# Per-head 64x64 key-value sums, and half of the first MLP's weight low parts on GpSimd

## The chip, the cores and the metric

One core of a Trainium2 chip runs the whole program. The metric is the device time of one execution in microseconds (us); less is better. The engines are called PE (TensorE's matmuls), PEld (its weight loads), DVE (VectorE), ACT (ScalarE), POOL (GpSimd) and SP (SyncE, which issues the DMAs).

## What is computed

Three stages follow each other: retention attention (linear attention with a decay per head, no softmax), an MLP with the activation h·cos(h), and a second, gated MLP behind an RMS norm.

```
scores = q @ k.T / sqrt(64)                    # 4 batches, 8 heads, 576 positions, 64 per head
ret    = (scores * gamma[h] ** (i - j) for i >= j, else 0) @ v
x      = ret, heads side by side                # 2304 tokens x 512
h      = x @ w_in                               # 512 -> 2048
x      = (h * cos(h)) @ w_out                   # 2048 -> 512
xn     = x / rms(x) * rms_g
out    = (silu(xn @ w_gate) * (xn @ w_val)) @ w_out2    # 512 -> 1536 -> 512
```

## The kernel before, in words

Each of the 4 batches is cut into 5 chunks of positions, four of 128 and one of 64, so there are 20 chunks, counted here from 0. A chunk is handled in two steps. `scores` (lines 238 to 253) scales the values on POOL (L243), makes the 8 heads' score blocks on PE (L248) and masks them on DVE (L251). `values` (lines 255 to 283) first adds the chunk's keys times values to a running sum in PSUM, `total` (L264, for the four full chunks of a batch); then it makes the output bank `po` from the running `state` and the queries (L269, from the second chunk on), copies the new sum into `state` on ACT (L274), adds each head's scores times values (L279), and takes `po` out of PSUM on DVE into `xall` (L282).

Heads go in pairs, since two heads of 64 fill 128 partitions. Before the change L264 multiplies the pair's 128 key columns by the pair's 128 value columns. Of each 128x128 result only the two 64x64 blocks on the diagonal are wanted, and the copy into `state` takes just these.

The first MLP works on f32 numbers split into a high and a low part (fp32r), three matmuls for one: hi·hi, hi·lo, lo·hi (`mm3`, lines 184 to 188). Its weights come as 16 blocks, each with 512 columns of `w_in` and 512 of `w_out`. A block is turned from two 32-bit words per number into f32 by `value1` to `value3` (L131 and L140 on ACT; L135, L136, L141, L142 on DVE), and split by `convert`: ACT writes the high part of all 1024 columns (L158), DVE the low part by a subtraction (the `w` instruction of L123, called by L159; L123 is the helper `minus`, and other subtractions have that line too: `xlo` for the MLP's input and `glo` for its middle). Each step of the first MLP has 12 matmuls into a hidden bank, the cosine gate (L413 and L416 on ACT, L414 and L420 on DVE, then `ghi` on ACT and `glo` on DVE), and 12 matmuls into the output banks three steps later.

The first 9 chunks' `values` come before the MLP's first step. The other chunks run between the MLP's first 8 steps, and the weight blocks are converted three steps ahead of their use. In this part a scheduler sets each engine's order by its own costs, so an edit here can move instructions that it doesn't name. Each engine then works strictly in the order that it was given. From the 16th step on the order on ACT, DVE and POOL is that of the code.

POOL has little else to do: 20 instructions of L243 in the attention and two `glo` much later.

Of the kernel before, what the change touches and what calls it, by code (L numbers as in the profile page):

```python
# [22 lines left out]
F32 = mybir.dt.float32  # L23
# [7 lines left out]
P = 128  # L31
B, H, S, D = 4, 8, 576, 64
# [5 lines left out]
NPAIR = H // 2  # L38
# [37 lines left out]
def body(ctx: ExitStack, tc, qkv, qkr, vr, w1, w2, rg, gq, gk, mask, out):  # L76
    nc = tc.nc
# [19 lines left out]
    psa = att.enter_context(tc.tile_pool(name="psa", bufs=1, space=PSUM, reuse_waits="tile"))  # L97
# [11 lines left out]
    def ps_tile():  # L109
        if "psh" not in late:  # L110
            return psa.tile([P, 512], F32, tag="g", bufs=3, name="g")
        taken[0] += 1
        return hidden_tile() if taken[0] % 2 else acc_tile(KC + taken[0] // 2 % 2)
# [8 lines left out]
    def minus(eng, dst, hi, src):  # L122
        eng.tensor_tensor(dst, src, hi.bitcast(F32), op=ALU.subtract)  # L123
# [6 lines left out]
    def value1(t, words):  # L130
        nc.scalar.activation(t.bitcast(F32), words[..., 1].bitcast(F32), AF.Abs)  # L131

    def value2(t):
        size = t.bitcast(F32)
        nc.vector.tensor_scalar(size, size, LEAST, LARGEST, op0=ALU.max, op1=ALU.min)  # L135
        nc.vector.tensor_scalar(t, t, 3, 0x3FFFFFF8, op0=ALU.logical_shift_left, op1=ALU.bitwise_and)  # L136

    def value3(t, words):
        low, high = words[..., 0], words[..., 1]
        nc.scalar.activation(low, low.bitcast(U32), AF.Copy, scale=2.0 ** -29)  # L140
        nc.vector.scalar_tensor_tensor(t, high, -2 ** 30, t, op0=ALU.bitwise_and, op1=ALU.bitwise_or)  # L141
        nc.vector.tensor_tensor(t, t, low, op=ALU.add)  # L142

    class Block:
# [7 lines left out]
        def convert(self, t):  # L152
            value1(t, self.raw)
            value2(t)
            value3(t, self.raw)
            self.w = self.where.tile([P, 2, 2, 512], F32R, tag="w", name="w")
            z = t.bitcast(F32)
            nc.scalar.copy(self.w[:, :, 0], z)  # L158
            minus(nc.vector, self.w[:, :, 1], self.w[:, :, 0], z)  # L159

        def parts(self, n):
            return self.w[:, n, 0, :], self.w[:, n, 1, :]
# [42 lines left out]
    ld, sc, total = {}, {}, {}  # L205
# [6 lines left out]
    state = ap1.tile([P, NPAIR, P], F32, name="state")  # L212
# [5 lines left out]
    def load(n):  # L218
# [14 lines left out]
        if 0 < n < NCH:  # L233
            gam.append(ap1.tile([P, NPAIR, width(c)], F32, name=f"gam{c}"))
            for p in range(NPAIR):
                nc.scalar.activation(gam[c][:, p, :], gam0[:, p, :width(c)], AF.Copy, scale=later[:, c, p:p + 1])

    def scores(n):
        b, c = chunks[n]
        w = width(c)  # L240
        kt, qt, vv, _ = ld[n]
        v3 = vv[:w].rearrange("p (h d) -> p h d", h=H)
        nc.gpsimd.tensor_tensor(v3, v3, vg_sb[:w, c, :].unsqueeze(2).to_broadcast([w, H, D]), op=ALU.mult)  # L243
        ps = [ps_tile().rearrange("p (h i) -> p h i", h=NPAIR) for _ in range(2)]
        for p in range(NPAIR):
            for hh in range(2):
                r = slice(hh * D, (hh + 1) * D)
                nc.tensor.matmul(ps[hh][:w, p, :w], kt[r, p, :], qt[r, p, :], start=True, stop=True)  # L248
        for hh in range(2):
            s = ap.tile([P, NPAIR, P], F32, tag=f"s{hh}", bufs=2, name=f"s{hh}")  # L250
            nc.vector.tensor_tensor(s[:w, :, :w], ps[hh][:w, :, :w],  # L251
                                    mask_sb[:w, :w].unsqueeze(1).to_broadcast([w, NPAIR, w]), op=ALU.mult)
            sc[n, hh] = s

    def values(n):
        b, c = chunks[n]
        w = width(c)
        _, qt, vv, kk = ld.pop(n)
        if c < NFULL:
            if c == 0:  # L260
                total[0] = psa.tile([P, NPAIR, P], F32, tag="st", name="total")
            for p in range(NPAIR):
                cs = slice(p * P, (p + 1) * P)
                nc.tensor.matmul(total[0][:, p, :], kk[:, cs], vv[:, cs], start=c == 0 and p == 0, stop=True,  # L264
                                 skip_group_check=True)
        po = ps_tile().rearrange("p (a i) -> p a i", a=NPAIR)
        if c > 0:
            for p in range(NPAIR):
                nc.tensor.matmul(po[:, p, :w], state[:, p, :], qt[:, p, :], start=p == 0, stop=False,  # L269
                                 skip_group_check=True)  # L270
        if c < NFULL:
            for hh in range(2):
                r = slice(hh * D, (hh + 1) * D)
                nc.scalar.copy(state[r, :, r], total[0][r, :, r])  # L274
        for p in range(NPAIR):
            for hh in range(2):
                h = 2 * p + hh
                r = slice(hh * D, (hh + 1) * D)
                nc.tensor.matmul(po[r, p, :w], vv[:w, h * D:(h + 1) * D], sc[n, hh][:w, p, :w],  # L279
                                 start=c == 0 and p == 0, stop=True, skip_group_check=True)  # L280
        t0 = b * S + c * P
        nc.vector.tensor_tensor(xall[:, :, t0:t0 + w], po[:, :, :w], gam[c], op=ALU.mult)  # L282
        del sc[n, 0], sc[n, 1]
# [16 lines left out]

    fetch(1)
    scores(0)
    for n in range(PRO):
        fetch(n + AHEAD)
        scores(n + 1)
        values(n)
        if n == 3:
            split_x(ORDER_A[0])
            blocks1[0].convert(temps())
# [315 lines left out]
    for i in range(LAST + LAG):  # L625
# [12 lines left out]
        if i < LAST:  # L638
            t, f = steps[i]
            ps = hidden(t, f)  # L640
            if f == NF1 - 1 and i + 1 < LAST:
                split_x(ORDER_A[ORDER_A.index(t) + 1])
            gate_cos(t, f, ps, (lambda: scores(more[0] + 1)) if more and more[0] + 1 < N else None,
                     nc.vector if i < NF1 or i >= 3 * NF1 or begun(i) is not None else nc.gpsimd,
                     piece_steps(begun(i), max(valued, default=None)) if begun(i) is not None or valued
                     else other_steps() if i >= LAST - NF1 else iter(range(5)))
        elif i >= LAST:
            for engine in "ADADDD":
                pull(engine)
        if i >= LAG:  # L650
            out_t(*steps[i - LAG])
        if more:
            values(more[0])
            if more[0] + 2 < N:
                scores(more[0] + 2)
            if len(more) > 1:
                values(more[1])
            chunk += len(more)
# [249 lines left out]
```

## Time and profile before

| what | value |
|---|---|
| median of 3 runs | 932.84 us (932.81 to 936.48) |
| the profiled execution, its own time | 929.44 us |
| its span in the profile | 927.7 us |
| PE busy, share of the span | 900.8 us, 97% |
| DVE busy | 619.5 us, 67% |
| ACT busy | 461.9 us, 50% |
| POOL busy | 28.5 us, 3% |
| granted TensorE clock | 1.00 (2.4 GHz) |

A busy PE is not a PE at its peak: matmuls overlap, and their ends are modelled. So for PE the starts of instructions say more than the busy time. An f32 matmul stands in the trace as two instructions: four matmuls of L264 are eight rows. Times inside the program are counted from the span's start.

### The profile page before, as it was taken

To read this page: it belongs to the slowest core of one execution; us is meant where nothing else is said; L and a number is where in the kernel's file an instruction comes from. 1 tells how busy PE (TensorE), PEld (TensorE's weight loads), DVE (VectorE), ACT (ScalarE), POOL (GpSimd) and SP (SyncE) were. 2 spreads that over 40 slices of the span, in tenths; PEclk is the share of its full clock that TensorE was granted. 3 is DMA by queue.
4 is the path that set the end of the run, shared out by engine and by line. 5 is a ranking of instruction groups with operands and counts; after the bars stand their busy time and mean duration, and the time that the engine had idled before them with its cause. 6 is when DMAs were issued, how large, how long until landed. Compare 5 with 4: busy or idle time off the path is not lost.

```text
span 927.7 us, 12893 instructions
## 1 busy us (share of the span) xinstructions
PE 900.8 (97%) x4996; PEld 790.4 (85%) x4996; DVE 619.5 (67%) x1022; ACT 461.9 (50%) x815; POOL 28.5 (3%) x27
## 2 busy tenths in 40 slices
PE   7989999999999999999998899999999999999998
PEld 6777888888887888988887799999888999999997
DVE  3999989678888887768656666675456446333332
ACT  4656566676556665367443444444432334322222
POOL 2321100000000000000000000000000000000000
PEclk9999999999999999999999999999999999999999
DMA  8956451035524443202044466666744555755531
GB/s 328 400 201 225 156 230 66 25 113 193 173 88 159 146 150 125 69 1 102 1 160 180 176 252 250 250 267 249 249 183 176 205 209 214 265 207 209 206 134 68
DMA packets 34732, 163.72 MB, mean 176 GB/s; under 512 B 4080, under 2 KB 5232, under 8 KB 23792
## 3 DMA queue, kind: packets, MB, share of 16 engines
q1 hardware_dynamic: 34672, 162.91, 48.6%
q8 instruction: 39, 0.64, 0.3%
q14 instruction: 21, 0.17, 0.1%
HBM read 123.57 MB, written 39.32 MB: 176 GB/s over the span
## 4 chain that ended last, share of the span: by engine, by line
PE 76%; DVE 16%; ACT 5%; issue 2%; DMA 1%; SPq 0%; ACTq 0%; DVEq 0%
PE h L738 27%; PE acc L710 15%; PE acc L186 8%; PE acc L187 7%; PE acc L188 7%; PE h L187 3%; PE h L188 3%; PE h L186 3%; DVE t L141 1%; DVE r L420 1%; DVE t L142 1%; DVE w L123 1%; DVE r L414 1%; DVE s L251 1%; DVE glo L123 1%
## 5 line engine op out<-in xcount | busy, mean ns | idle before, releaser
L738 PE MATMUL h<-w 128*128 128x384 f32 x1224 | 230.0, 337 | 8.7 <-DVE sg L758 4.2
L738 PEld LDWEIGHTS h<-w 128*128 128x128 f32 x1224 | 215.0, 188 | 16.6 <-DVE sg L758 5.5
L710 PE MATMUL acc<-w,shi 128*128 128x512 f32 x432 | 134.3, 392 | 0.0
L186 PE MATMUL acc<-ghi,w 128*128 128x512 f32 (+1 forms) x320 | 117.3, 373 | 2.8 <-ACT xall L612 1.7
L745 ACT COPY s<-h 128x384 f32<-128x384 f32 x108 | 51.8, 479 | 133.3 <-PE h L738 133.2
L187 PE MATMUL acc<-glo,w 128*128 128x512 f32 (+1 forms) x320 | 117.6, 369 | 0.1
L188 PE MATMUL acc<-ghi,w 128*128 128x512 f32 (+1 forms) x320 | 117.3, 368 | 0.0
L710 PEld LDWEIGHTS acc<-w,shi 128*128 128x128 f32 x432 | 80.1, 188 | 13.5
L758 DVE TENSOR_TENSOR sg<-s,h 128x384 f32<-128x384 f32 x54 | 29.9, 553 | 87.5 <-PE h L738 48.2
L416 ACT ACTIVATE r<-r,half_pi 128x512 f32<-128x512 f32 (+1 forms) x80 | 54.5, 681 | 66.0 <-DVE r L414 65.6
L710 PE MATMUL acc<-w,slo 128*128 128x512 f32 x216 | 85.4, 396 | 0.0
L123 DVE TENSOR_TENSOR glo<-r,ghi 128x512 fp32r<-128x512 f32 (+1 forms) x78 | 49.8, 639 | 33.2 <-ACT ghi L422 31.3
L186 PEld LDWEIGHTS acc<-ghi,w 128*128 128x128 f32 x320 | 59.4, 188 | 14.5 <-ACT xall L612 2.7
L770 ACT CAST shi<-v 128x384 fp32r<-128x384 f32 x72 | 37.1, 515 | 68.6 <-DVE v L766 68.6
L422 ACT CAST ghi<-r 128x512 fp32r<-128x512 f32 (+1 forms) x80 | 46.2, 577 | 48.2 <-DVE r L420 47.0
L188 PEld LDWEIGHTS acc<-ghi,w 128*128 128x128 f32 x320 | 60.3, 188 | 10.1
L187 PEld LDWEIGHTS acc<-glo,w 128*128 128x128 f32 x320 | 60.3, 188 | 10.0 <-DVE glo L123 0.3
L765 DVE TENSOR_TENSOR v<-s,h 128x384 f32<-128x384 f32 x54 | 29.8, 552 | 53.5 <-PE h L738 40.9
L123 DVE TENSOR_TENSOR slo<-v,shi 128x384 fp32r<-128x384 f32 x72 | 40.1, 557 | 36.7 <-ACT shi L770 36.7
L738 PE MATMUL h<-b,w 128*128 128x384 f32 x288 | 56.7, 337 | 0.0
L187 PE MATMUL h<-xlo,w 128*128 128x512 f32 (+1 forms) x148 | 54.3, 367 | 0.1
L188 PE MATMUL h<-xhi,w 128*128 128x512 f32 (+1 forms) x148 | 54.2, 366 | 0.0
(104 smaller groups left out, 1517.1 us busy)
## 6 DMA issues: line engine op xcount, KB each, us to landing
w<-s SPq DMA_DIRECT2D x24, 1024.0 KB, 4.8
raw<-w_dram SPq DMA_DIRECT2D x36, 512.0 KB, 4.2
w<-w SPq DMA_DIRECT2D x18, 1024.0 KB, 5.1
w<-s SPq DMA_DIRECT2D x24, 768.0 KB, 6.5
raw<-w_dram SPq DMA_DIRECT2D x16, 1024.0 KB, 6.7
x<-qkv_dram SPq DMA_DIRECT2D x15, 1024.0 KB, 9.3
s<-w SPq DMA_DIRECT2D x12, 1024.0 KB, 4.8
s<-w SPq DMA_DIRECT2D x12, 768.0 KB, 3.6
```

The lines of the kernel that those rows point to most:

```text
L123: eng.tensor_tensor(dst, src, hi.bitcast(F32), op=ALU.subtract)
L186: nc.tensor.matmul(dst, a[0], b[0], start=start, stop=False)
L187: nc.tensor.matmul(dst, a[0], b[1], start=False, stop=False)
L188: nc.tensor.matmul(dst, a[1], b[0], start=False, stop=stop)
L416: nc.scalar.activation(r, r, AF.Sin, bias=half_pi, scale=1.0)
L422: nc.scalar.copy(hi, r)
L710: nc.tensor.matmul(acc, (hi, hi, lo)[k][:, c], w[:, u, (0, 1, 0)[k], :], start=start and u == 0 and k == 0, stop=stop and u == 1 and k == 2)
L738: nc.tensor.matmul(bank, a[:, wp], xp[:, c], start=start and kc == 0 and n == 0, stop=kc == 1 and n == 2, skip_group_check=True)
L745: nc.scalar.copy(t, alpha)
L758: nc.vector.tensor_tensor(t, s, bank, op=ALU.add)
L765: nc.vector.tensor_tensor(t, s, bank, op=ALU.add)
L770: nc.scalar.copy(hi, t)
```

## The change

Two edits. The sum of keys and values is made head by head: eight matmuls of 64 key columns by 64 value columns, each into its own half of the partitions, in place of four of 128 by 128; `total` shrinks to 64 columns per pair, and the copies into `state` read it accordingly. And of each weight block's low part DVE makes only the `w_in` half, POOL the `w_out` half.

```diff
@@ class Block, convert @@
             nc.scalar.copy(self.w[:, :, 0], z)
-            minus(nc.vector, self.w[:, :, 1], self.w[:, :, 0], z)
+            minus(nc.vector, self.w[:, 0, 1], self.w[:, 0, 0], z[:, 0])
+            minus(nc.gpsimd, self.w[:, 1, 1], self.w[:, 1, 0], z[:, 1])
...
+    half = lambda hh: slice(hh * D, (hh + 1) * D)
...
@@ values @@
-                total[0] = psa.tile([P, NPAIR, P], F32, tag="st", name="total")
+                total[0] = psa.tile([P, NPAIR, D], F32, tag="st", name="total")
             for p in range(NPAIR):
-                cs = slice(p * P, (p + 1) * P)
-                nc.tensor.matmul(total[0][:, p, :], kk[:, cs], vv[:, cs], start=c == 0 and p == 0, stop=True,
-                                 skip_group_check=True)
+                for hh in range(2):
+                    h = 2 * p + hh
+                    cs = slice(h * D, (h + 1) * D)
+                    nc.tensor.matmul(total[0][half(hh), p, :], kk[:, cs], vv[:, cs], start=c == 0 and p == 0,
+                                     stop=True, skip_group_check=True)
...
-                nc.scalar.copy(state[r, :, r], total[0][r, :, r])
+                nc.scalar.copy(state[half(hh), :, half(hh)], total[0][half(hh)])
```

The new code has three lines more ahead of `scores` and two more in `values`, so L243 becomes L246, L264 becomes L269, L269 becomes L274, L282 becomes L285; L123 to L142 keep their numbers.

The scheduler's order moves with it, at three places.

**POOL, the attention and the first MLP's weights.** `x` is a chunk's values being scaled, `w` a weight block's low part. Before, the second half of POOL's attention work:

```order
12 L243 TENSOR_TENSOR x<-x,gk_sb 128x512 x4
13 L243 TENSOR_TENSOR x<-x,gk_sb 64x512
14 L243 TENSOR_TENSOR x<-x,gk_sb 128x512 x4
15 L243 TENSOR_TENSOR x<-x,gk_sb 64x512
16 L123 TENSOR_TENSOR glo<-r,ghi 128x512 x2
```

With the change:

```order
18 L246 TENSOR_TENSOR x<-x,gk_sb 128x512
19 L123 TENSOR_TENSOR w<-t,w 128x512
20 L246 TENSOR_TENSOR x<-x,gk_sb 128x512 x2
21 L123 TENSOR_TENSOR w<-t,w 128x512
22 L246 TENSOR_TENSOR x<-x,gk_sb 64x512
23 L123 TENSOR_TENSOR w<-t,w 128x512
24 L246 TENSOR_TENSOR x<-x,gk_sb 128x512 x2
25 L123 TENSOR_TENSOR w<-t,w 128x512
26 L246 TENSOR_TENSOR x<-x,gk_sb 128x512 x2
27 L123 TENSOR_TENSOR w<-t,w 128x512
28 L246 TENSOR_TENSOR x<-x,gk_sb 64x512
29 L123 TENSOR_TENSOR w<-t,w 128x512 x7
```

Of the 16 `w` instructions nine now stand between the scalings, so that a later chunk's scaling is queued behind a weight block, and seven come after the last chunk's.

**DVE, around the last three attention chunks.** `xall` with `gam_142`, `gam_149` and `gam_159` are the outputs of chunks 17, 18 and 19. Before:

```order
132 L123 TENSOR_TENSOR w<-t,w 128x2x512
133 L123 TENSOR_TENSOR glo<-r,ghi 128x512
134 L135 TENSOR_SCALAR t<-t 128x1024
135 L136 TENSOR_SCALAR t<-t 128x1024
136 L282 TENSOR_TENSOR xall<-g,gam_142 128x4x128
137 L251 TENSOR_TENSOR s_1183<-g,mask_sb 64x4x64
138 L251 TENSOR_TENSOR s_1185<-g,mask_sb 64x4x64
139 L141 SCALAR_TENSOR_TENSOR t<-raw,t 128x1024
140 L142 ISA t<-raw,t 128x2048
141 L282 TENSOR_TENSOR xall<-g,gam_149 128x4x128
```

With the change:

```order
134 L423 TENSOR_TENSOR r<-g,r 128x512
135 L141 SCALAR_TENSOR_TENSOR t<-raw,t 128x1024
136 L123 TENSOR_TENSOR glo<-r,ghi 128x512
137 L142 ISA t<-raw,t 128x2048
138 L285 TENSOR_TENSOR xall<-g,gam_142 128x4x128
139 L254 TENSOR_TENSOR s_1252<-g,mask_sb 64x4x64
140 L254 TENSOR_TENSOR s_1254<-g,mask_sb 64x4x64
141 L123 TENSOR_TENSOR w<-t,w 128x512
142 L285 TENSOR_TENSOR xall<-g,gam_149 128x4x128
```

A block's L141 and L142 have moved from behind chunk 17's output to ahead of it, and a `w`, now of 512 columns, from behind chunk 18's output to ahead of it.

**PE, the first two chunks.** `total` is the sum of keys and values. Before:

```order
12 L279 MATMUL g<-s_138,x 64x128
13 L264 MATMUL total<-x 128x128 x2
14 L248 MATMUL g<-x 128x128 x8
15 L264 MATMUL total<-x 128x128 x2
16 L269 MATMUL g<-x,state 128x128 x4
```

With the change:

```order
12 L282 MATMUL g<-s_138,x 64x128
13 L269 MATMUL total<-x 64x64 x5
14 L251 MATMUL g<-x 128x128 x8
15 L269 MATMUL total<-x 64x64 x3
16 L274 MATMUL g<-x,state 128x128 x4
```

The place is the same; four matmuls of 128 by 128 have become eight of 64 by 64. In both orders 156 matmuls of the first MLP stand ahead of the last chunk's last attention matmul.

## Rows read from the trace of the kernel before

**Rows 1.** Windows: busy us and instructions per engine, clock, DMA share, GB/s.
```profile
21.00:120.00 99.00, 93.80 (x856) 77.84 (x854) 96.36 (x124) 58.76 (x83) 20.97 (x16) 1.00 0.63 239
130.00:165.00 35.00, 35.00 (x156) 28.93 (x155) 34.26 (x44) 24.27 (x31) 0.00 (x0) 1.00 0.35 136
```

**Rows 2.** Timeline of PE, the last chunks: start us, us, what, idle before.
```profile
115.38 1.05 PE L264 MATMUL total<-x 128*128 128x128 f32 x8
116.27 1.06 PE L269 MATMUL g<-x,state 128*128 128x128 f32 x8
117.25 1.09 PE L279 MATMUL g<-s,x 128*64 128x128 f32 x16
118.28 0.68 PE L248 MATMUL g<-x 64*64 64x64 f32 x16
...
120.43 1.16 PE L269 MATMUL g<-x,state 128*128 128x128 f32 x8 [0.38 <-DVE xall L282]
...
129.07 0.68 PE L279 MATMUL g<-s,x 64*64 64x64 f32 x16
129.68 0.50 PE L186 MATMUL acc<-ghi,w 128*128 128x512 f32 x1
```

**Rows 3.** Chain that ended last, in order of time: start us, us, what.
```profile
14.83 0.68 PE total L264 x4
...
58.46 0.68 PE g L248 x8
...
83.15 1.09 PE total L264 x8
...
86.20 0.69 DVE xall L282
```

**Rows 4.** Timeline of DVE while POOL is idle, 111 to 119 us.
```profile
111.93 1.21 DVE L123 TENSOR_TENSOR w<-t,w 128x1024 fp32r<-128x1024 f32 x1
113.06 1.21 DVE L142 CUSTOM_DVE_ANT_0 t<-raw,t 128x2048 uint16<-128x2048 uint16 x1
...
117.76 0.68 DVE L123 TENSOR_TENSOR glo<-r,ghi 128x512 fp32r<-128x512 f32 x1
118.36 0.69 DVE L135 TENSOR_SCALAR t<-t 128x1024 f32<-128x1024 f32 x1
```

**Rows 5.** Timeline of DVE and POOL, 99.5 to 105 us.
```profile
99.93 1.37 POOL L243 TENSOR_TENSOR x<-x,gk_sb 128x512 f32<-128x512 f32 x1 [12.26 <-DMA x<-qkv_dram]
...
100.31 2.07 DVE L123 TENSOR_TENSOR w<-t,w 128x1024 fp32r<-128x1024 f32 x1
...
102.30 1.21 DVE L142 CUSTOM_DVE_ANT_0 t<-raw,t 128x2048 uint16<-128x2048 uint16 x1
102.42 2.00 POOL L243 TENSOR_TENSOR x<-x,gk_sb 128x512 f32<-128x512 f32 x1 [1.12 <-DVE w L123]
...
103.44 0.68 DVE L414 SCALAR_TENSOR_TENSOR r<-r,g 128x512 f32<-128x512 int32 x1
```

**Rows 6.** Groups of 0 to 180 us (count | busy us, mean ns); L243's min/median/max ns.
```profile
L141 DVE SCALAR_TENSOR_TENSOR t<-raw,t 128x1024 int32<-128x1024 int32 x16 | 21.3, 1329 | 0.2
...
L142 DVE CUSTOM_DVE_ANT_0 t<-raw,t 128x2048 uint16<-128x2048 uint16 x16 | 20.4, 1277 | 0.1
L123 DVE TENSOR_TENSOR w<-t,w 128x1024 fp32r<-128x1024 f32 x16 | 20.4, 1273 | 1.3 <-ACT w L158 1.1
...
L136 DVE TENSOR_SCALAR t<-t 128x1024 int32<-128x1024 int32 x16 | 12.6, 785 | 0.2
...
L123 DVE TENSOR_TENSOR xlo<-xall,xhi 128x512 fp32r<-128x512 f32 x8 | 6.2, 810 | 0.7 <-ACT xhi L180 0.7
...
L243 POOL TENSOR_TENSOR x<-x,gk_sb x20: 1037/1068/1997, 7.1 to 109.9; 128x512 f32<-128x512 f32 x16, 64x512 f32<-64x512 f32 x4
```

**Rows 7.** Timeline of ACT and PE, 88 to 96 us: a weight block and chunk 15.
```profile
88.92 1.05 ACT L158 CAST w<-t 128x1024 fp32r<-128x1024 f32 x1 [0.72 <-DVE t L142]
...
95.88 1.16 PE L264 MATMUL total<-x 128*128 128x128 f32 x8
```

More of the change, by code (lines that the diff above doesn't have):

```diff
@@ L272, in values @@
             for hh in range(2):
-                r = slice(hh * D, (hh + 1) * D)
-                nc.scalar.copy(state[r, :, r], total[0][r, :, r])
+                nc.scalar.copy(state[half(hh), :, half(hh)], total[0][half(hh)])
         for p in range(NPAIR):
@@ L277, in values @@
                 h = 2 * p + hh
-                r = slice(hh * D, (hh + 1) * D)
-                nc.tensor.matmul(po[r, p, :w], vv[:w, h * D:(h + 1) * D], sc[n, hh][:w, p, :w],
+                nc.tensor.matmul(po[half(hh), p, :w], vv[:w, h * D:(h + 1) * D], sc[n, hh][:w, p, :w],
                                  start=c == 0 and p == 0, stop=True, skip_group_check=True)
```

## The prediction

> **What bounds the kernel now.** I read the windows first, then the two timelines of PE and DVE, then the chain of waits, and last the groups of instructions of the first 180 us. Both edits touch only the attention and the first MLP's weight blocks; no instruction of either lies behind the first MLP's first 16 steps. In the windows the reader is to see three stretches. From 21 to 120 us DVE is busy 96.4 of 99 us, and PE 93.8: both are nearly full [rows 1]. From 130 us on PE is busy all the time, 35.00 of 35 [rows 1]. So the end of the program moves with one thing: the moment at which the last attention chunks let PE go on. The two orders have the same 156 MLP matmuls ahead of the last chunk's last attention matmul, so what PE has left after that point is the same.
>
> That moment hangs on DVE: chunk 18's first matmul on PE stands 0.38 us for the output that DVE copies out for chunk 17 [rows 2]. The chain of waits lies on PE from 58.46 us to 86.20, where DVE takes it over [rows 3], and on DVE in the stretches ahead of and behind that one, from 21 and to 120 us. The old sums of keys and values (L264) are in it in seven places, the first and the last of which are shown [rows 3]: two before 21 us with 8 instructions, five in PE's stretch with 24. These 32 are the work of four chunks of 16.
>
> **Part 1, what DVE saves.** Starts are the measure, since the shown durations overlap: a low part of 1024 columns holds DVE from 111.93 to 113.06, 1.13 us; one of 512 columns (`glo`, same operation and types) from 117.76 to 118.36, 0.60 us [rows 4]. Each block thus saves DVE 0.53 us. Up to chunk 17's output both orders hold ten blocks' low parts: -5.3 us. But the new order has one block's L141 and L142 ahead of that output which stood behind it before; L142 shows the same 1.21 us as the whole low part [rows 4], so I take 1.13 for each: +2.3 us. Up to chunk 18's output the orders differ by the low parts alone, ten whole ones (11.3 us) against eleven halves (6.6 us): -4.7 us.
>
> **Part 2, what POOL's new work costs DVE.** On POOL the operation takes at least 1.04 us for 128x512, and the longest L243 took 2.00 [rows 6]. POOL has the time: it is busy 21 of 99 us [rows 1]. The price is on DVE. At 99.93 us POOL starts a scaling that lasts until 101.30; DVE's low part starts at 100.31 and takes 2.07 us in place of 1.21, about as much longer as the two overlap [rows 4, 5]. At 102.30 it is the other way round: DVE is first with L142, and POOL's scaling takes 2.00 us [rows 5]. L414, which reads one input from PSUM, runs 0.68 us in the midst of that scaling, not slowed [rows 5]. So a DVE instruction that takes both inputs from SBUF and a POOL instruction exclude each other, and one that reads PSUM passes.
>
> How much does one POOL instruction cost DVE on the average? Against undisturbed durations (1.21 us for the large ones, 0.69 for L136 as for L135, 0.68 for `xlo` as for `glo` [rows 4]) the means are longer by 0.12 us for L141, 0.07 for L142, 0.06 for the low part, 0.10 for L136 (16 of each) and 0.13 for `xlo` (8 of them) [rows 6]: 1.9 + 1.1 + 1.0 + 1.5 + 1.0 = 6.5 us. Of the 20 scalings 16 lie after 21 us, where DVE is full [rows 1], so one costs 0.41 us. The bounds for a `w` on POOL are 0 (only PSUM readers beside it) and 1.04 (none). I take 0.41, since these rows are of the same engine, shape and stretch. Ten blocks up to chunk 17's output: +4.1 us (0 to 10.4); eleven up to chunk 18's: +4.5.
>
> So DVE is at -5.3 + 2.3 + 4.1 = +1.1 us at chunk 17's output and at -4.7 + 4.5 = -0.2 at chunk 18's. Which of them sets the pace I can't tell from the rows, so I take the middle, +0.4.
>
> The Trainium skill speaks against this half of the change: SBUF — State Buffer, section Who interferes with whom, says that VectorE and GpSimd share a port pair under an exclusive lock, so that a VectorE instruction with two SBUF inputs and a GpSimd one that reads SBUF block each other entirely. By that rule the trace agrees (2.07 us against 1.21), and it reads as a full 1.04 us per block wherever no PSUM reader is beside it, which is the second rival below.
>
> **Part 3, the sums of keys and values.** Before, a chunk's L264 holds PE from 115.38 to 116.27, 0.89 us [rows 2]. The new form is 16 instructions with 64 weight columns, 64 moving columns and all 128 rows, two heads in turn into the two halves of the partitions. The nearest row is L279 of a short chunk: 16 instructions, 64 weight and 64 moving columns, the same two halves, but 64 rows; with the step to the next work it takes from 129.07 to 129.68, 0.61 us [rows 2]. The other neighbour has 128 rows and 64 weight columns, but 128 moving columns: 117.25 to 118.28, 1.03 us [rows 2]. The change per chunk lies between -0.28 and +0.14 us; I take -0.28, since what differs in that row (the number of rows summed over) doesn't set the time in the full-size forms either: L264 and L269, 128 rows both, and L279's pair of halves all stand near 0.11 us per 128 columns [rows 2]. For the four chunks that lie on the chain: -1.1 us. For all 16 it would be -4.5, but under DVE's stretches PE then only waits longer.
>
> The Trainium skill has a rule on this: TensorEngine Tiling (Array Packing), section Key Properties, says that changing the tiling mode drains TensorE. The trace agrees in part: from L269 to L279, which goes from whole to half columns, it is 0.98 us where L264 to L269 is 0.89 [rows 2], so 0.09 per change; the 0.61 us above already has one such step in it.
>
> **Part 4, what costs nothing.** POOL's queue: a chunk's scaling now stands behind a block's `w`, which waits for ACT's high part. The tightest place is chunk 15. ACT ends the high part at 89.97 us, so with `w` and the scaling at 1.04 us each the values are ready at about 92.1; PE first uses them at 95.88 [rows 7]. If that cover of 3.8 us went, the sum of chunk 15 and its output would be late by as much as ACT is. The `w_out` half is needed three steps after the `w_in` half. The seven blocks after the attention run under a full PE [rows 1]. The copies into `state` have the same size.
>
> **The sum.** +0.4 - 1.1 = -0.7 us. The profiled execution took 929.44 us, so 928.7; on the median of the runs, 3.4 us above it, 932.1 us. About 0.5% (4.7 us) is what a measurement of this kernel can tell from no change.
>
> **Rivals.**
> 1. *PE sets the pace, and the gain is had in full.* For: PE is nearly as full as DVE from 21 to 120 us, and the scheduler has dealt the work anew on both. Then all 16 chunks count, -4.5 us, and if half of the lock's cost falls beside PSUM readers, DVE's sum at chunk 17's output is -5.3 + 2.3 + 2.05 = -1.0 and PE's waits for it shrink by as much: about -5.5, that is 927.3 us. Against: DVE's stretches in the chain are longer, some 71 us of the first 120 against PE's 28 from 58.46 to 86.20 [rows 3].
> 2. *The lock costs more than the low part was worth.* Every `w` on POOL starts the moment ACT's high part is done, when DVE's next work is mostly the next block's L135 to L142, all reading SBUF. At a full 1.04 us per block: -5.3 + 2.3 + 10.4 - 1.1 = +6.3 us, 939.1 us. It decides from 0.88 us per block on, where the sum passes +4.7. For: the pairs at 100 and 102 us. Against: the mean over 16 scalings is less than half of that.
> 3. *The halves don't go side by side.* Then 16 instructions at L264's 0.11 us each take 1.78 us a chunk, +0.89 us: +3.6 us for the four chunks on the chain, more as PE becomes the bound; about +5 with DVE's +0.4, 937.8 us. Against: L279's halves do go side by side [rows 2].
>
> **How the numbers follow.** The forecast has 0.55, rival 1 0.26, rival 2 0.15, rival 3 0.04. The forecast's own range, with the lock at 0.15 to 0.75 us per block and Part 3 at both ends, is 929 to 937. The whole reaches down to 925.5 to hold rival 1, and up to 938, short of rival 2. Faster by over 0.5% has 0.27 (rival 1 and a little of the forecast's edge), slower by over 0.5% 0.18, no change 0.55.
>
> **What would show it.** In the profile of the changed kernel: `w` on DVE near 0.60 us from start to start, and L141, L142, L135 and L136 with larger means than before by 0.41 us per POOL instruction in sum; a chunk's sum of keys and values at about 0.6 us on PE; DVE still full from 21 to 120 us; chunk 19's output within 2 us of 129.8; PE full from there on. The prediction is wrong if chunk 19's output comes 4 or more us earlier or later, if PE waits for POOL, or if PE loses time after 130 us, where I see none.

## The result, and the profile after

The changed kernel is slower: 941.28 us (median of 6 runs, 938.47 to 942.26) against 932.83 us for the kernel before beside it (6 runs, 930.24 to 936.48). The ratio of the runs is 1.0084, with a 95% interval of 1.0064 to 1.0104: +7.8 us (6.0 to 9.7), where no change (932.1 us) was forecast. The time is above the range, and its sign is the one that had 0.18.

The profiled execution took 942.26 us, its span is 940.1 us. It is 1.0 us above the median of its kernel, and that of the kernel before was 3.4 us below its own, so some 4.4 us of the distance between the two profiles is the spread of the runs. I read it in the order in which the kernel before was read. First the windows of the changed kernel (busy us and instructions of PE, PEld, DVE, ACT and POOL, then clock, DMA share, GB/s):

```profile
21.00:120.00 99.00, 88.41 (x887) 71.03 (x887) 89.94 (x116) 55.41 (x77) 35.65 (x24) 0.91 0.65 238
40.00:80.00 40.00, 33.69 (x297) 27.18 (x298) 32.03 (x42) 22.42 (x30) 12.09 (x8) 0.85 0.49 180
142.00:177.00 35.00, 35.00 (x156) 28.98 (x155) 33.62 (x40) 22.02 (x29) 8.30 (x5) 1.00 0.34 135
```

The same 40 us of the kernel before:

```profile
40.00:80.00 40.00, 36.91 (x310) 30.61 (x311) 38.87 (x50) 24.69 (x33) 7.97 (x6) 1.00 0.64 239
```

The last of these three rows stands against the second of [rows 1]: once the attention is over PE is full and nothing more is lost. The loss lies ahead of it. From 21 to 120 us DVE was busy 96.4 us before [rows 1] and is busy 89.9 now: it has 6.4 us more without work, all of it and more from 40 to 80 us (1.1 us idle before, 8.0 now). PE's granted clock is 0.85 there, so part of the stretch ran at 1.2 GHz. The last outputs of the attention stand on DVE at

```profile
130.57 0.67 DVE L285 TENSOR_TENSOR xall<-g,gam 128x512 f32<-128x512 f32 x1
133.53 0.69 DVE L285 TENSOR_TENSOR xall<-g,gam 128x512 f32<-128x512 f32 x1 [0.95 <-PE g L282]
141.09 0.42 DVE L285 TENSOR_TENSOR xall<-g,gam 128x256 f32<-128x256 f32 x1
```

Chunk 19's was at 129.8 us before, so it is 11.3 us late, and the span 12.4 us longer. Chunk 5's output is 5.4 us late, chunk 6's 5.1, chunk 7's 9.5 (67.79 against 58.33), chunk 8's 10.4; then the distance shrinks to 5.6 us at chunk 13 and grows again to 11.3. So a loss is there by chunk 8, far ahead of the chunks 17 and 18 at which the prediction counted; the outputs alone don't say that the last chunk's delay is this one. Here is DVE between chunk 6's and chunk 7's outputs in the changed kernel (timeline: start us, us, what, idle before):

```profile
49.59 0.69 DVE L285 TENSOR_TENSOR xall<-g,gam 128x512 f32<-128x512 f32 x1 [0.38 <-PE g L282]
...
50.91 2.20 DVE L141 SCALAR_TENSOR_TENSOR t<-raw,t 128x1024 int32<-128x1024 int32 x1
53.15 1.95 DVE L142 CUSTOM_DVE_ANT_0 t<-raw,t 128x2048 uint16<-128x2048 uint16 x1
...
58.70 1.42 DVE L136 TENSOR_SCALAR t<-t 128x1024 int32<-128x1024 int32 x1
60.15 1.23 DVE L141 SCALAR_TENSOR_TENSOR t<-raw,t 128x1024 int32<-128x1024 int32 x1
61.29 0.68 DVE L417 SCALAR_TENSOR_TENSOR r<-r,g 128x512 f32<-128x512 int32 x1
61.89 1.22 DVE L142 CUSTOM_DVE_ANT_0 t<-raw,t 128x2048 uint16<-128x2048 uint16 x1
63.03 1.28 DVE L254 TENSOR_TENSOR s<-g,mask_sb 128x512 f32<-128x512 f32 x2
64.23 0.68 DVE L123 TENSOR_TENSOR w<-t,w 128x512 fp32r<-128x512 f32 x1
64.83 0.68 DVE L423 TENSOR_TENSOR r<-g,r 128x512 f32<-128x512 f32 x1
67.79 0.69 DVE L285 TENSOR_TENSOR xall<-g,gam 128x512 f32<-128x512 f32 x1 [2.28 <-PE g L282]
```

and in the kernel before:

```profile
50.68 0.68 DVE L251 TENSOR_TENSOR s<-g,mask_sb 128x512 f32<-128x512 f32 x1
...
52.41 1.54 DVE L136 TENSOR_SCALAR t<-t 128x1024 int32<-128x1024 int32 x1
53.87 0.68 DVE L251 TENSOR_TENSOR s<-g,mask_sb 128x512 f32<-128x512 f32 x1
54.47 1.60 DVE L141 SCALAR_TENSOR_TENSOR t<-raw,t 128x1024 int32<-128x1024 int32 x1
```

The two `s` are chunk 7's masked scores. Before, they stood one ahead of and one just behind a block's L136; now they stand together behind L136, L141 and L142 of that block, at 63 us. PE's next instruction waits for the first of them, and PE works in order; its timeline:

```profile
55.75 0.50 PE L189 MATMUL g<-xhi,w 128*128 128x512 f32 x1 [1.73 <-DVE w L123]
...
63.76 2.07 PE L274 MATMUL g<-x,state 128*128 128x128 f32 x8 [4.58 <-DVE s L254]
65.77 1.98 PE L282 MATMUL g<-s,x 128*64 128x128 f32 x16
```

PE stands 4.58 us for the masks, and then runs the same eight and sixteen matmuls at half speed: 2.07 and 1.98 us, where L269 took 1.06 and L279 1.09 [rows 2]. DVE in turn stands 2.28 us for chunk 7's bank. Each waits for the other; in the prediction's picture DVE, being full, had no such wait.

What the two edits do by themselves is also there. The sum of a chunk is now one row of 16, and the next work starts 0.61 us behind it:

```profile
49.51 0.69 PE L269 MATMUL total<-x 128*64 128x64 f32 x16
50.12 0.50 PE L187 MATMUL acc<-ghi,w 128*128 128x512 f32 x1
```

And POOL's new work collides with DVE's (POOL and DVE, 32 to 40 us; the scalings were queued behind the first `w`, which waited 6.93 us for ACT):

```profile
32.58 1.38 POOL L123 TENSOR_TENSOR w<-t,w 128x512 fp32r<-128x512 f32 x1 [6.93 <-ACT w L158]
32.74 1.77 DVE L136 TENSOR_SCALAR t<-t 128x1024 int32<-128x1024 int32 x1
33.92 4.38 POOL L246 TENSOR_TENSOR x<-x,gk_sb 128x512 f32<-128x512 f32 x3
34.43 1.52 DVE L123 TENSOR_TENSOR w<-t,w 128x512 fp32r<-128x512 f32 x1
35.88 1.53 DVE L123 TENSOR_TENSOR xlo<-xall,xhi 128x512 fp32r<-128x512 f32 x1
37.33 2.06 DVE L141 SCALAR_TENSOR_TENSOR t<-raw,t 128x1024 int32<-128x1024 int32 x1
```

L136 takes 1.77 us, two subtractions 1.5 and L141 2.06, where undisturbed ones take 0.69, 0.68 and 1.21. So three suspects stood: the collisions on DVE (theory L), a clock that falls because the shorter sums leave PE idle (theory C), and the order in which the scheduler put the work (theory O).

### The profile page after: what moved, and what is told of

Read it like the earlier page. It is cut to its first block, busy times and chain, and to the rows that moved or that the text cites. A ratio compares the mean times of both kernels' runs of the same rounds, so it can differ in the third digit from the quotient of the medians.

```text
span 940.1 us, 13184 instructions
## 1 busy us (share of the span) xinstructions
PE 906.3 (96%) x5124; PEld 792.3 (84%) x5124; DVE 622.3 (66%) x1022; ACT 462.3 (49%) x815; POOL 56.7 (6%) x43
## 4 chain that ended last, share of the span: by engine, by line
PE 77%; DVE 15%; ACT 4%; issue 2%; DMA 1%; SPq 0%; ACTq 0%; DVEq 0%
PE h L741 26%; PE acc L713 15%; PE acc L187 7%; PE acc L188 7%; PE acc L189 7%; PE h L187 3%; PE h L189 3%; PE h L188 3%; PE g L282 2%; PE g L251 1%; PE g L274 1%; DVE t L141 1%; DVE r L423 1%; DVE t L142 1%; DVE glo L123 1%
## 5 line engine op out<-in xcount | busy, mean ns | idle before, releaser
L123 DVE TENSOR_TENSOR glo<-r,ghi 128x512 fp32r<-128x512 f32 (+1 forms) x78 | 52.8, 677 | 33.3 <-ACT ghi L425 31.4
L123 DVE TENSOR_TENSOR slo<-v,shi 128x384 fp32r<-128x384 f32 x72 | 40.1, 556 | 37.0 <-ACT shi L773 37.0
```

## The experiments

**Each half alone, each in the order that the scheduler gave it.** One run has the new sums only (`convert` as before), one POOL's halves only (sums as before), one the sums and POOL's halves for the blocks 11 to 15 alone:

```diff
-            minus(nc.vector, self.w[:, 0, 1], self.w[:, 0, 0], z[:, 0])
-            minus(nc.gpsimd, self.w[:, 1, 1], self.w[:, 1, 0], z[:, 1])
+            if len(blocks1) and self in blocks1 and blocks1.index(self) >= 11:
+                minus(nc.vector, self.w[:, 0, 1], self.w[:, 0, 0], z[:, 0])
+                minus(nc.gpsimd, self.w[:, 1, 1], self.w[:, 1, 0], z[:, 1])
+            else:
+                minus(nc.vector, self.w[:, :, 1], self.w[:, :, 0], z)
```

Sums only, expected:

> The sums of keys and values head by head, as in the change; the low parts of the weights all on DVE, as before. Theory L (GpSimd's low parts lock DVE out in bursts, PE stands idle for it, and the lower clock follows from the idle PE): without them this is 929 to 934 us, a clock of 0.995 or more, DVE's lock cost near the 6.9 us of before. Theory C (the shorter sums leave PE with too little to do, the clock falls, and that is the loss): 936 to 942 us with a clock of 0.985 to 0.99, as the change.

POOL's halves only, expected:

> The sums as before, 128 by 128; half of each weight block's low part on GpSimd, as in the change. Theory L: nearly all of the loss is here, 938 to 943 us, DVE's lock cost near the 15.9 us of the change, PE idle for several us between 30 and 65 us. Theory C: within 2 us of before, 931 to 935, and a clock of 1.00.

POOL's halves late only, expected:

> As the changed kernel, but GpSimd makes the half low parts only of the last five weight blocks (11 to 15), after the attention; the matmul order is that of e1_sums. Theory L: the lock hurts only where DVE is what PE waits for, so this is within 1.5 us of e1_sums. If the lock costs anywhere, 2 to 4 us slower than e1_sums. Theory C: as e1_sums, whatever that is.

Measured: sums only 937.00 us against 934.26, ratio 1.0042 [1.0017, 1.0067]; POOL's halves only 944.79, 1.0109 [1.0082, 1.0137]; late halves 935.65, 1.0021 [0.9997, 1.0045]. The parts don't add up: POOL's halves alone cost more than the whole change, and the sums, which take work away, cost time. Theory L explains the one and theory C the other, but neither explains both, and each run had a new order on DVE, ACT and PE besides. So these runs can't tell an edit from its order; the next ones keep the order.

**POOL's work added, nothing else moved.** In the traces of the next two runs DVE, ACT and PE issue in the order of the kernel before (first 250 us). In the first, POOL makes a spare copy of the half in every block, and DVE still makes both halves:

```diff
             minus(nc.vector, self.w[:, :, 1], self.w[:, :, 0], z)
+            spare = cvp.tile([P, 512], F32R, tag="spare", bufs=1, name="spare")
+            minus(nc.gpsimd, spare, self.w[:, 1, 0], z[:, 1])
```

In the second, POOL is as long at work, but nearly all of it only writes:

```diff
+            spare = cvp.tile([P, 512], F32R, tag="spare", bufs=1, name="spare")
+            minus(nc.gpsimd, spare[:, :1], self.w[:, 1, 0, :1], z[:, 1, :1])
+            nc.gpsimd.memset(spare[:, 1:].bitcast(F32), 0.0)
+            nc.gpsimd.memset(spare[:, 1:].bitcast(F32), 0.0)
```

> The kernel before, and in every MLP block one more subtraction on GpSimd, of the output weights' half into a spare tile that nobody reads; VectorE still makes both low halves, and no other engine gets an instruction more or in another place. Theory L (GpSimd's subtractions hold VectorE up when it starts on the same block, TensorE then waits, and its clock falls): VectorE's rows that overlap a GpSimd row grow together by 7 to 12 us as in the changed kernel (6.9 us before, 15.9 there), the last chunk's output comes 4 to 9 us late and the time is 937 to 942 us, although VectorE is spared nothing here and TensorE's work is as before. Theory C (what costs is the new shape of the sums alone, by which TensorE has gaps and falls to the lower clock): within 1.5 us of the kernel before.

> As the run with a spare subtraction, but GpSimd's extra work per block is one subtraction of a single column and two fills of 511 columns with zero into the spare tile: it stands in the same place of GpSimd's queue, but reads nothing for most of its time. Theory L with the wait as a matter of GpSimd's reading operations: VectorE's overlap excess grows by under 2 us, time within 2 us of the kernel before (931 to 935). A rival Q (what costs is the place in GpSimd's queue, ahead of the scalings of the chunks, not the lock): as slow as the run with the spare subtraction, 937 to 942. Theory C: within 1.5 us of the kernel before.

Measured: the spare subtraction 940.16 us against 932.17, ratio 1.0077 [1.0044, 1.0110], or +7.2 us (4.1 to 10.3). The fills 933.00, ratio 1.0012 [0.9993, 1.0031]. The groups of the spare subtraction's run, 0 to 180 us (count | busy us, mean ns):

```profile
L123 DVE TENSOR_TENSOR w<-t,w 128x1024 fp32r<-128x1024 f32 x16 | 23.3, 1458 | 1.1 <-ACT w L158 1.1
L141 DVE SCALAR_TENSOR_TENSOR t<-raw,t 128x1024 int32<-128x1024 int32 x16 | 22.7, 1418 | 0.2
...
L136 DVE TENSOR_SCALAR t<-t 128x1024 int32<-128x1024 int32 x16 | 13.8, 863 | 0.2
L123 DVE TENSOR_TENSOR glo<-r,ghi 128x512 fp32r<-128x512 f32 x15 | 13.3, 883 | 1.9 <-ACT ghi L424 1.8
```

with `glo` in the kernel before at

```profile
L123 DVE TENSOR_TENSOR glo<-r,ghi 128x512 fp32r<-128x512 f32 x17 | 11.9, 700 | 2.9 <-ACT ghi L422 2.9
```

Against [rows 6] `w` grew by 2.9 us, L141 by 1.4, L136 by 1.2 and `glo` by 15 times 0.18 us, or 2.7; L135, L142 and `xlo` add some 0.4. That is 8.6 us for 16 operations: 0.54 us each, and 0.65 if the 7.2 us are shared among the eleven that lie ahead of the last chunk. In the run with the fills POOL was as long at work per block (0.98 + 0.56 + 0.53 us in the means of its groups, against 2.02), at the same place of its queue, and the time stayed within the noise; `w` on DVE is as in the kernel before:

```profile
L123 DVE TENSOR_TENSOR w<-t,w 128x1024 fp32r<-128x1024 f32 x16 | 20.1, 1257 | 1.4 <-ACT w L158 1.3
```

So what costs is that the subtraction reads, not where it stands: rival Q falls. The Trainium skill has this too: SBUF — State Buffer, section Who interferes with whom, says that a VectorE instruction with two SBUF inputs contends with a GpSimd one that reads SBUF, not with one that only writes it. Here the runs agree, with +7.2 us (4.1 to 10.3) against +1.1 (-0.7 to 2.9).

**The same work in a new order.** The sums as 16 instructions that take PE nearly as long as the 8 did (64 weight columns by the old 128 moving ones), and the new sums with a filler that gives PE more than its work back (0.52 to 0.60 us a chunk in its trace, where the sums saved 0.28). The second diff is against the changed kernel, and leaves out that `convert` is as before:

```diff
-                nc.tensor.matmul(total[0][:, p, :], kk[:, cs], vv[:, cs], start=c == 0 and p == 0, stop=True,
-                                 skip_group_check=True)
+                for hh in range(2):
+                    r = slice(hh * D, (hh + 1) * D)
+                    nc.tensor.matmul(total[0][r, p, :], kk[:, (2 * p + hh) * D:(2 * p + hh + 1) * D], vv[:, cs],
+                                     start=c == 0 and p == 0, stop=True, skip_group_check=True)
```

```diff
-                total[0] = psa.tile([P, NPAIR, D], F32, tag="st", name="total")
+                both = psa.tile([P, 2, NPAIR, D], F32, tag="st", name="total")
+                total[0], total[1] = both[:, 0], both[:, 1].rearrange("p a d -> p (a d)")
+            nc.tensor.matmul(total[1], kk[:, :P], vv[:, :2 * P], start=c == 0, stop=True, skip_group_check=True)
```

> The kernel before with each pair's sum taken as two matmuls of 64 weight columns by the same 128 moving columns, into the two halves of the pair's tile, so a chunk has 16 sums as in the changed kernel but the bank, the width and the two reads of the total stay. Theory C: pairs of these matmuls go side by side as the narrow ones did, about 1.0 us for the 16 against 0.9 for the 8 before, so TensorE has no more gaps than before, and the time is within 1.5 us of the kernel before at a granted clock over 0.99. A rival O (the order in which the scheduler puts the work changes with the number of sums, and that is what costs): 2 to 5 us slower, as the sums alone were.

> The run with the sums per head alone, and in every chunk one more matmul into the free half of the total's bank, 256 moving columns that nobody reads, about 0.25 us at the full clock: it gives TensorE back the work that the narrow sums take away. Theory C: the clock comes back over 0.99 and the time to within 1.5 us of the kernel before, although there is more work than with the sums alone (937.0). Rival O (the order): stays 2 to 5 us slower. Theory that only TensorE's amount of work counts: 20 times 0.25 us above the sums alone, 940 to 942.

Measured: 940.91 us, ratio 1.0094 [1.0066, 1.0122], and 941.54 us, 1.0089 [1.0054, 1.0123]. Theory C falls as the cause of the whole: a loss of this size needs neither shorter work on PE nor a low part on POOL. (The granted clock is low in these runs too, 0.990 and 0.992 on the average against 0.995, so what falls is that the shorter sums lower it, not that a low clock takes part.) In the first the pairs do go side by side (a chunk's 16 hold PE from 64.70 to 65.72 us, 1.02 us, against 0.89 before). Theory O had the direction right and the size (2 to 5 us) too small by half. The place is the same as in the changed kernel; PE in the run with the old columns:

```profile
59.88 2.08 PE L271 MATMUL g<-x,state 128*128 128x128 f32 x8 [5.29 <-DVE s L251]
61.89 1.98 PE L281 MATMUL g<-s,x 128*64 128x128 f32 x16
```

Chunk 7's masks are late here too, without any of POOL's halves, and PE falls to half speed.

**The change in the order of before.** The scheduler was now bound: each instruction got an edge, without a wait, to the one that stood ahead of it on its engine in the kernel before, by a table of numbers in program order (VectorE, ScalarE, TensorE; a pair's two sums stand where its one stood). In the traces of the three runs, up to 250 us, DVE, ACT and PE issue in the order of before, the sums apart. POOL, which isn't bound, has the changed kernel's order but for one or two places.

```diff
+    for engine, text in ORDER_BEFORE.items():
...
+                for i in groups[k]:
+                    if last is not None:
+                        tc.add_manual_dep(i, last.name, info, reason="order of the kernel before")
+                    last = i
```

Sums only:

> The sums per head alone (GpSimd makes no low part), but VectorE, ScalarE and TensorE issue everything in the order of the kernel before: edges without a wait pin it, and each pair's two narrow sums stand where its one sum stood. Theory C (the narrow sums give TensorE less to do, it has gaps, its clock falls): 2 to 5 us slower than the kernel before, with a granted clock under 0.99, as with the sums alone in their own order (937.0 against 934.3). Theory O (the sums cost nothing themselves; the new order of the work round them does): 0.3 to 1.5 us faster, since 16 chunks have each 0.42 us less on TensorE and only those on the chain pay; 930.7 to 932 if the kernel before is at 932.2.

POOL's halves only:

> GpSimd makes the low halves of the output weights, the sums as before, and VectorE, ScalarE and TensorE issue everything in the order of the kernel before; GpSimd's own order is that of the changed kernel. Theory L (GpSimd's subtractions hold VectorE up and bring its results late, whatever the order): 3 to 7 us slower, 935 to 939, with VectorE's excess over GpSimd rows at 13 us or more (6.9 before). Theory O (the order costs the time): VectorE is spared 16 times 0.6 us, some 10 of these before the last chunk, and gives back about 4 to 8 in the overlaps: between 4 us faster and 0.5 us slower, 928 to 932.5.

Both:

> The whole change, with VectorE, ScalarE and TensorE in the order of the kernel before. Theory O: 927 to 932.5, level with the kernel before or faster, and 9 to 12 us under the changed kernel. Theory L: 934 to 939, within 1.5 us of the run with GpSimd's halves alone in that order. Theory C: 937 or more, above the run with GpSimd's halves alone by the 2 to 5 us of the sums.

Measured, against 933.26 us (35 runs):

| in the order of before | us | ratio |
|---|---|---|
| sums per head | 933.79 | 1.0011 [0.9993, 1.0028] |
| POOL's halves | 934.90 | 1.0013 [0.9996, 1.0031] |
| both | 935.86 | 1.0027 [1.0010, 1.0044] |
| both, in the changed kernel's order (above) | 941.28 | 1.0084 [1.0064, 1.0104] |

So the two edits in an unmoved order cost +2.5 us (0.9 to 4.1), and they do add up. The other 5.3 of the 7.8 us (2.9 to 7.7) came with the order. The sums fit neither text: theory C wanted at least 2 us of loss, theory O a gain. POOL's halves lie just under theory L's 935 and above theory O's 932.5; both together (935.86) are in L's range and out of the other two. So O is right on where most of the loss is, but not that the edits pay, and L is right that the overlaps stay in either order. The excess of DVE's rows over their undisturbed length is nearly as large with both edits in the old order as in the changed kernel (17.1 and 18.9 us in the first 200 us, 7.7 before; each row of over 0.3 us against the 30th percentile of its kind), while the time differs by 5 us. DVE in the run with both, with chunk 7's masks and output at their old places:

```profile
54.67 0.68 DVE L254 TENSOR_TENSOR s<-g,mask_sb 128x512 f32<-128x512 f32 x1
...
57.91 0.68 DVE L254 TENSOR_TENSOR s<-g,mask_sb 128x512 f32<-128x512 f32 x1
...
61.97 0.68 DVE L287 TENSOR_TENSOR xall<-g,gam 128x512 f32<-128x512 f32 x1
```

**Where in the order.** The order cut in two at chunk 7's output: old ahead of it and new behind it, and the other way round. Only the table differs, and with it a few rows of POOL's order. Its first line for DVE, new order and old, in numbers of program order (55 and 56 are chunk 7's masks, 49 to 52 the block's L135 to L142; `48+4` is 48 to 51):

```diff
-    "0+14 22+2 14+3 24+2 17 27+2 18 29 39 19 40 26 20 41 21 42 31 30 32 35 33 44 36+2 34 38 45+3 43 48+4 54 52 55+2 "
+    "0+14 22+3 14+3 25 17+2 27 19 28 20 26 21 29 31 39+3 30 32 35 33 42 36 34 37+2 44+4 43 49 55 48 50 56 51 54 52 "
```

> The whole change; VectorE, ScalarE and TensorE issue in the order of the kernel before up to chunk 7's output, and from there on in the order of the changed kernel. If the loss is made where VectorE's masks and outputs stand behind a block's conversion (theory OH: the order up to chunk 7's output), chunk 7's output is back at 61 to 63 us (67.8 in the changed kernel, 62.0 with the order of before throughout), the last chunk's output at 134 to 137, and the time 934.5 to 937. If the loss is spread over the whole order (theory OS), the gain is had at chunk 7 and lost again behind it: last output at 139 to 142, 939 to 941.

> The counterpart: the order of the changed kernel up to chunk 7's output, and from there on that of the kernel before. Theory OH: chunk 7's output at 66 to 69 us, the last chunk's output at 139 to 142, 939 to 941.5, as the changed kernel. Theory OS: about half of the loss, 937 to 939.

Measured, against 933.03 us: old order ahead 936.78 us, ratio 1.0039 [1.0023, 1.0055], chunk 7's output at 61.20 us and chunk 19's at 135.90; new order ahead 940.39 us, 1.0085 [1.0059, 1.0110], chunk 7's output at 64.3 and chunk 19's at 139.47. The windows of the one and of the other from 40 to 80 us:

```profile
40.00:80.00 40.00, 35.76 (x297) 29.92 (x299) 37.06 (x47) 22.54 (x31) 12.93 (x9) 0.87 0.60 229
```

```profile
40.00:80.00 40.00, 34.81 (x319) 28.43 (x316) 31.24 (x40) 23.33 (x31) 12.75 (x9) 0.87 0.51 189
```

DVE is busy 37.06 us with the old order ahead and 31.24 with the new one, where PE stands for chunk 7's masks again and falls to half speed:

```profile
60.24 2.08 PE L276 MATMUL g<-x,state 128*128 128x128 f32 x8 [3.00 <-DVE s L254]
```

Of the order's 5.3 us about 4.2 belong to the stretch up to chunk 7's output (1.0084 less 1.0039, give or take 2.4); with the old order behind it, it is 5.4 (1.0085 less 1.0027). The order behind accounts for about 1, which is within the noise. That it is the two masks, and not another of the moves on DVE, ACT and PE in this stretch, is read from the timelines; no run moved the masks alone. Chunk 7's output in the second run came at 64.3 us, earlier than the 66 to 69 expected, while its time is the changed kernel's. So not all of that stretch's cost shows in this one output: the run's chunk 8 (69.1 us) is 3.5 us behind the run with both edits in the old order (65.6).

**A later start of the conversions.** `CONV_LEAD = 2` in place of 3 in the kernel before, in the order that the scheduler then gave:

> The kernel before with a conversion begun two MLP steps ahead of its use in place of three (one number); sums and low parts as before. VectorE is the engine that is full from 21 to 120 us, so a block's 6 us of conversion that moves from there to after the last chunk should bring the chunks forward: 3 to 6 us faster, 926 to 929. If instead only the order counts, any new order, this one too, costs 2 to 9 us as the others did.

Measured: 932.04 us against 933.26, ratio 0.9988 [0.9972, 1.0004]. Not the 3 to 6 us: it is 1.1 us, between 2.6 faster and 0.4 slower. It shows that a new order isn't bad as such, and that taking a block's conversion off DVE (10 low parts ahead of the last output in place of 11) doesn't bring the last chunk forward by as much: it came at 130.4 us in the profile, against 129.8 before. No run gave a version that clearly beats the kernel before.

## Why the prediction was wrong

**What bounds the kernel: this failed, and with it the sum.** The step was: DVE and PE are nearly full from 21 to 120 us, so the end moves with the work that DVE has ahead of the last outputs. It was right as a reading of [rows 1], but not as a law for another order. I let DVE be full in the new order too, and compared the orders only at chunks 17 and 18; the cost of the order elsewhere stood at nothing in the sum, without a reason. DVE has 6.4 us less of work in those 99 us, and it is none the earlier (the last output comes 11.3 us late, past the 4 us that the prediction named as its sign of being wrong): it waits for PE, and PE for it. The longest of these waits stands at chunk 7, where two masks had moved behind a block's L136 to L142; the table of the order has that move, and the prediction left it out. Cost of the new order: some 5.3 us, 4.2 of them up to chunk 7's output. How much of it the masks alone make, and how much the lower clock that comes with PE's waits, stays open.

**Part 1, what DVE saves: right in size.** In the changed kernel a `w` of 512 columns holds DVE from 64.23 to 64.83 us, 0.60 us as taken, so a block saves 0.53. The run with the spare subtraction (+7.2 us) and the one with POOL's halves in the old order (+1.2) differ by what DVE is spared, 6.0 us (2.5 to 9.5), against 5.3 for ten blocks and 5.8 for eleven. The +2.3 us for the moved L141 and L142 was a term of the new order at chunk 17 and wasn't measured by itself.

**Part 2, the lock: right in kind, too small.** 0.41 us per operation was taken, with bounds of 0 and 1.04; it is 0.54 by DVE's rows, and 7.2 us in time against the 4.1 and 4.5 of the prediction. Two things were missing. `glo`, with two inputs from SBUF, pays as well (0.88 us on the average instead of 0.70), and I had left it out. And rival 2's argument held in part: a `w` starts the moment ACT is done, when DVE begins its own half of the same block or the next block's chain. The rival's full price of 1.04 us did not come. Nor are two inputs from SBUF the whole condition, as the prediction had it: L136 has a single one, and took 1.77 us beside POOL's `w` where 0.69 is undisturbed. Rival 2's time of 939.1 was the nearest of the four, but for the wrong reason: with the lock at 7.2 us in place of 4.3, and the rest of the sum as it stood, the forecast would have been +2.2 us, that is 935.0, near the 935.86 of both edits in the old order.

**Part 3, the sums: the size right to the hundredth, the gain not had.** 0.61 us a chunk was read from the neighbour row; the changed kernel shows 49.51 to 50.12. But in the old order the sums give +1.0 us (-0.7 to +2.6) where -1.1 was expected. So rival 3 is out, and rival 1 too: what PE saved did not reach the end of the program.

**Part 4: it held for the places that it names.** PE never waits for POOL in the first 150 us of the changed kernel, and nothing is lost once PE is full. It left out the first `w` in POOL's queue: POOL waits 6.93 us for ACT there, with three scalings behind it, which then run in a row beside DVE's L136, `w`, `xlo` and L141.

**The sum**, with the terms as measured: edits in the old order +2.5, order up to chunk 7 +4.2, order behind it +1.1 (within the noise), together +7.8 us. No rival had this: each of them keeps one engine busy throughout and prices its work, and none has two engines that wait for each other.

## What to carry to other kernels

Where a scheduler sets the order, an edit's price has two parts, that of its instructions and that of the order it triggers, and the second can be the larger: compare the two orders from the first moved row on, and ask of each producer (here two masks) that moved behind a long chain who waits for it. Full engines are a fact about one order; when two engines feed each other, a late row on one makes idle time on both. And to price an edit, bind the order first (or add the work to an idle engine, with the others unmoved), then let the scheduler go.

## What the runs showed of the hardware

**The granted clock fell behind waits, with the short sums and with the old ones.** In the changed kernel's first chunks PE stood 1.53 us and 1.79 us for two loads, and ran the 16 score matmuls of a chunk at half speed:

```profile
9.82 0.69 PE L269 MATMUL total<-x 128*64 128x64 f32 x16 [1.53 <-DMA x<-qkv_dram]
12.30 2.08 PE L251 MATMUL g<-x 64*128 64x128 f32 x16 [1.79 <-DMA x<-qkv_dram]
```

and before, with 1.31 and 1.27 us of waiting, it stayed at full speed:

```profile
8.89 1.13 PE L264 MATMUL total<-x 128*128 128x128 f32 x8 [1.31 <-DMA x<-qkv_dram]
11.29 1.16 PE L248 MATMUL g<-x 64*128 64x128 f32 x16 [1.27 <-DMA x<-qkv_dram]
```

2.08 against 1.16 us is 1.2 against 2.4 GHz: the granted clock from 12 to 16 us is 0.50 in the one and 1.00 in the other. The shorter sum isn't what decides it. POOL's halves alone, with the old sums, fell as well, and the sums alone, with the short ones, did not in this stretch:

```profile
12.51 2.08 PE L249 MATMUL g<-x 64*128 64x128 f32 x16 [0.83 <-DMA x<-qkv_dram]
11.41 1.16 PE L250 MATMUL g<-x 64*128 64x128 f32 x16 [1.72 <-DMA x<-qkv_dram]
```

Nor does this early stretch cost much: `CONV_LEAD = 2`, in whose profile the clock is 0.50 from 12 to 16 us too, is as fast as the kernel before.

**One kernel's runs differ by the clock.** The 35 runs of the kernel before in one batch go from 928.96 us at a granted clock of 1.000 to 936.97 at 0.991; a line through them gives 0.72 us per 0.001. The sums in the old order had 0.9908 on the average, the kernel before 0.9949; by that line this is 3.0 us, and at an equal clock the sums would be some 2 us faster, near what Part 3 hoped for. (A line through the twelve runs of the sums gives 0.46 per 0.001, and some 1 us.) That the clock takes the gain away is an inference from this line, not shown by a run that holds the clock fixed. The same line put to the changed kernel, 0.9877 on the average against this 0.9949, gives about 5 of its 7.8 us, and to both edits in the old order, 0.9913, all of their 2.5 us. So a good part of the loss may come by way of the clock; waits and clock go together here, and which of them carries the order's 5.3 us no run separates.

**A writing POOL costs nothing that these runs can tell.** Fills of 511 columns on POOL, 0.53 and 0.56 us on the average and two in every block, left DVE's `w` at 1257 ns (1273 before), and the time at a ratio of 1.0012 (0.9993 to 1.0031).
